# First layer-norm tiles on two engines, and a new token order, in a fused S4 and feed-forward kernel

## The chip, the cores and the metric

The kernel runs on one core of a Trainium2 chip. The metric is device microseconds from launch to end, the median of several executions; lower is better. A profiled execution gives the trace that the views below are read from. Engines are named as in the profile: PE is TensorE (matmul), PEld its weight loads, DVE is VectorE, ACT is ScalarE, POOL is GpSimd, SP is SyncE, which here only issues DMAs. Every engine runs its own instructions in program order and waits in place for what the next one needs.

## The reference

A block of 2048 tokens of width 512 is normalised. One branch is a state-space convolution (S4) along the tokens, the other a feed-forward network with a hidden width of 1792. The second, through SiLU, gates the first:

```python
xn = _layernorm(x, axis=-1)
s = _A_ref(xn, A_re, A_im, B_re, B_im, C_re, C_im, log_dt, Dskip)   # y = conv(xn, K) + xn * Dskip
g = _silu(_B_ref(xn, w1, b1, w2, b2))                               # gelu(xn w1 + b1) w2 + b2
return x + s * g
...
dt = jnp.exp(log_dt)[:, None]
P = jnp.exp((dt * A)[:, :, None] * l[None, None, :])                # A, B, C complex, 512 x 128
K = jnp.einsum("dn,dnl,dn->dl", Cc, P, dt * Bc).real                # 512 x 2048
```

The convolution goes through a Fourier transform over twice the length.

## The kernel before

**Tiling.** Tokens are taken in tiles of 2 x 128 rows (`ln_load`, `ln_begin`), two tiles to a group of 512 tokens. There are four such groups. The hidden width is 14 blocks of 128, in two halves of 7 (`FA`), so the feed-forward network has 56 steps, one per group and block (`steps`). All matmuls of the network are done in a three-part split: each operand is a rounded high part and a low rest, and high x high, high x low and low x high are added up.

**The layer norm of a group.** VectorE takes mean and variance of each row tile (`ln_stat`, token LS). The inverse square root is worked out by arithmetic on 128x4 numbers (`ln_rsqrt`, line 366; token LR), and VectorE scales each 128x512 row tile (`ln_scale`, line 381; token LC). PE turns it (`ln_turn`, TF), ScalarE rounds the high part `xh` (`ln_high`, TH), and VectorE forms the low part `xl` (`ln_low`, TL). For group 0 all this stands in `prologue`, for the others in the token order.

**The feed-forward steps.** For step j: F.j.0 and F.j.1 are six matmuls each into one of two PSUM buffers named `f1` (`first_half`, lines 287 to 289; step 0 is `first_start`, line 298, and stands in the prologue). G.j is Gelu in place on ScalarE (line 302), H.j the rounding to `hh` on ScalarE (line 307), and R.j the rest `hl` on VectorE (line 313), the last reader of the PSUM buffer. S.j.i, four of them, are three matmuls each into the sums `z` (lines 323 to 325): `hh` x high weight, `hh` x low weight, `hl` x high weight. Weights are loaded by W and WB into a ring of six staging slots; WS.f.0 and WS.f.1 round the high parts on ScalarE, WS.f.2 and WS.f.3 form the low parts on VectorE (line 266), or on GpSimd where a third number 1 is given.

**The S4 kernel's parameters.** Each P.b token takes the next step of the generator `params(b)` for a quarter of the channels. Step 1 (for b = 0 in the prologue) loads six arrays. Step 2 is six products on GpSimd, ending in `wr` and `wi` (lines 519 to 524). Step 3 is two Abs on ScalarE (527, 528). Step 4 is six operations on VectorE (531 to 537). Step 5 is an arc tangent on ScalarE, step 6 ten and more operations on GpSimd, steps 7 to 9 more on VectorE, step 10 a store to memory, from which the tables' loads (KL, `lh`) and then PE's phase products (A, line 617) take them. The time step `dt`, the exponential of a 512-vector, is worked out by `timestep` (lines 491 to 505), 24 small dependent operations on GpSimd. It stands in the prologue, ahead of all P tokens, and `dt` is used from step 7 on.

**The rest.** A, B, C, Z, N, E, Q, U, UD make the convolution kernel, in 32 pieces, beside the feed-forward steps. Behind them come the transforms over four channel quarters (F1, FO, S2, SP, PR, CB, BK, BO, VT, LA), the gate (GM, GA, and for the last quarter SW, SO, LT, GT, AT) and the stores (OS, OT). In `combine`, `gate_add` and `rows_add` a trailing 1 or its absence chooses between VectorE and GpSimd; in `gen_round`, `back_out`, `first_out` and `ln_high` between VectorE and ScalarE.

**What sets the order.** The program is written out under manual scheduling: `prologue()` first, then the 1603 tokens of `ORDER` one after the other. Each engine's queue is the subsequence of the instructions that fall to it. So a token that waits for another engine holds everything behind it on its own engine.

```python
    with tc.manual_schedule():
        prologue()
        for tok in ORDER.split():
            kind, *args = tok.split(".")
            acts[kind](*map(int, args))
```

Of the kernel before, what the change touches and what calls it, by code (L numbers as in the profile page):

```python
# [54 lines left out]
TF.2.1 B.0.1 C.0 S.4.0 WS.6.0 TH.2.1 TF.3.0 WS.6.1 P.0 TL.2.1 WS.6.2 LS.5.0 WS.5.1 S.4.1 P.1 A.1 F.5.0 F.5.1
B.1.1 P.0 S.4.2 TH.3.0.1 TL.3.0 P.1 C.1 TF.3.1 S.3.3 N.0.0 G.5 LD.2 LD.3 P.0 S.4.3 H.5 TH.3.1 LS.4.0 R.5
KL.2.0 LS.5.1 TL.3.1 F.6.0 LS.4.1 KL.0.1 BB F.6.1 F.7.0 WS.6.3 WS.5.3 LR.4 LK.1 KL.1.1 KL.3.0 Z.0 N.0.1
S.5.0 S.5.1 KL.2.1 F.7.1 G.6 A.2 E.0.0 H.6 N.1.0 N.1.1 S.5.2 R.6 F.8.0 WB.8 G.7 LC.4 Z.1 E.0.1 H.7 S.6.0
E.0.2 F.8.1 O.0.0 E.1.0 S.6.1 B.2.1 S.5.3 R.7 G.8 S.6.2 H.8 E.1.1 S.7.0 F.9.0 C.2 LD.4 KL.3.1 Z.2 O.0.1 A.3
R.8 S.6.3 N.2.0 F.9.1 KL.4.0 G.9 O.0.2 S.7.1 E.1.2 H.9 S.8.0 B.3.1 S.8.1 P.1 C.3 LK.0 TF.4.0 N.2.1 O.0.3  # L60
S.7.2 S.8.2 Q.0 R.9 LC.5 TH.4.0 E.2.0 TL.4.0 TF.4.1 E.2.1 S.7.3 E.2.2 TH.4.1 S.8.3 N.3.0 S.9.0 KL.5.0 F.10.0
U.0 P.1 N.3.1 Z.3 S.9.1 LL.6 KL.4.1 A.4 F.10.1 KL.5.1 B.4.1 TL.4.1 G.10 S.9.2 E.3.0 F.11.0 LD.5 F.11.1 P.1
E.3.2 H.10 W.10 G.11 S.9.3 C.4 R.10 A.5 TF.5.0 H.11 S.10.0 E.3.1 TH.5.0 B.5.1 R.11 LS.6.0 S.10.1 C.5 Z.4
N.4.0 OK.0 KL.6.0 N.5.0 KL.7.0 TL.5.0 F.12.0 P.1 F.12.1 S.10.2 G.12 H.12 S.11.0 Z.5 S.11.1 TF.5.1 R.12 N.4.1
Q.1 P.1 S.12.0 P.1 P.1 S.10.3 U.1 KL.6.1 N.5.1 TH.5.1 P.1 F.13.0 E.4.0 LL.7 S.12.1 P.2 TL.5.1 F.13.1 E.5.0
S.11.2 F.14.0 S.11.3 G.13 F.14.1 E.4.2 E.5.1 S.12.2 H.13 R.13 UD.0 P.1 S.12.3 S.13.0 F.15.0 E.4.1 KL.7.1
LS.7.0 A.6 B.6.1 UD.1 F.15.1 E.5.2 G.14 S.13.1 Z.6 LS.7.1 H.14 O.1.0 C.6 G.15 R.14 N.6.0 H.15 LS.6.1 S.13.2
S.13.3 A.7 B.7.1 O.1.1 P.1 O.1.3 F.16.0 F.16.1 KL.8.0 C.7 S.14.0 N.6.1 R.15 P.2 Z.7 O.1.2 S.14.1 S.15.0 LR.6
F.17.0 S.14.2 Q.2 OK.1 F.17.1 E.6.0 G.16 LC.7 H.16 R.16 S.14.3 LC.6 U.2 S.16.0 KL.8.1 S.15.1 N.7.0 E.6.1
# [1097 lines left out]
```

## Time and profile before

| | |
|---|---|
| median of 3 runs | 530.98 us (530.38 to 534.08) |
| profiled execution | 529.94 us |
| its span, first to last instruction | 528.0 us |
| TensorE clock granted, mean | 0.996 |
| VectorE, ScalarE, GpSimd busy | 441.9, 373.2, 242.5 us |

A row of the timeline or of the groups has the start (timeline), the duration in us, the engine, the line of the kernel, the operation, what it writes and reads, sizes, and in brackets how long its engine stood idle before it and what ended that. A row of busy time by stretches has the stretch, its length, then busy time and instruction count of PE, PEld, DVE, ACT and POOL, then the granted clock of TensorE (1.00 is full), the busy share of the DMA engines and GB/s. A row of the waits has the waiting instruction, what it waited for, the total in us, how often, and the longest. A row of the chain of waits has start, duration and what the chain ran through. Instruction ends of pipelined matmuls are modelled, so distances between starts are the better measure for them.

### The profile page before, as it was taken

How to read it: one execution, taken by the hardware profiler on the slowest of the kernel's cores; microseconds unless marked ns; L12 is line 12 of the kernel's file. 1: busy time of each engine (PE TensorE's matmuls, PEld its weight loads, DVE VectorE, ACT ScalarE, POOL GpSimd, SP SyncE). 2: the span in 40 equal slices, each digit the busy share in tenths (PEclk: the TensorE clock that was granted, in tenths of full speed). 3: DMA queues.
4: the chain of work that ended last, by engine and by line, in shares of the span. 5: the costliest groups of instructions: out<-in, count | busy, mean ns of one | idle time of the engine just before them, and what ended most of it. 6: DMA issues, size and time to landing. Idle time of an engine off the chain costs nothing.

```text
span 528.0 us, 16480 instructions
## 1 busy us (share of the span) xinstructions
PE 513.2 (97%) x6931; PEld 417.1 (79%) x6931; DVE 441.9 (84%) x695; ACT 373.2 (71%) x530; POOL 242.5 (46%) x343
## 2 busy tenths in 40 slices
PE   6999999999999999999999999999999999999994
PEld 6786777877777777777777787777888998998972
DVE  5999999999999898999877867988455599788886
ACT  2689888977978898997697898998644543343321
POOL 5637379084531848927345157621303112733250
PEclk9999999999999999999999999999999999999998
DMA  8858823437167182624435155949489457573656
GB/s 224 272 176 276 309 90 135 149 110 269 33 221 253 54 242 72 228 89 127 157 107 196 39 179 117 253 118 115 151 284 187 129 184 122 155 189 88 171 145 165
DMA packets 106345, 86.84 MB, mean 164 GB/s; under 512 B 40974, under 2 KB 84640, under 8 KB 106272
## 3 DMA queue, kind: packets, MB, share of 16 engines
q1 hardware_dynamic: 104736, 84.74, 55.4%
q10 hardware_dynamic: 1472, 1.05, 0.8%
q8 instruction: 54, 0.88, 0.7%
q14 instruction: 19, 0.16, 0.1%
q0 software_dynamic: 64, 0.01, 0.0%
HBM read 52.23 MB, written 33.55 MB: 162 GB/s over the span
## 4 chain that ended last, share of the span: by engine, by line
PE 91%; DVE 3%; DMA 3%; ACT 1%; SPq 1%; issue 0%; ACTq 0%; DVEq 0%
PE s L938 11%; PE z L323 10%; PE f L287 10%; PE z L325 10%; PE z L324 9%; PE f L288 9%; PE f L289 9%; PE s L915 6%; PE kg L678 6%; PE sa L975 6%; PE ph L617 2%; DMA w2s<-in_B_w_dram 2%; PE y L1036 1%; DMA x<-in_A_u_dram 1%; PE xT L403 1%; DMA out_dram<-xb 0%
## 5 line engine op out<-in xcount | busy, mean ns | idle before, releaser
L323 PE MATMUL z<-w2h,hh 128*128 128x512 f32 x224 | 92.0, 411 | 0.0
L287 PE MATMUL f<-xh,w1h 128*128 128x512 f32 x220 | 88.9, 404 | 0.3 <-DVE hl L313 0.2
L325 PE MATMUL z<-w2h,hl 128*128 128x512 f32 x224 | 88.6, 396 | 0.0
L324 PE MATMUL z<-w2l,hh 128*128 128x512 f32 x224 | 88.5, 395 | 0.0
L639 POOL TENSOR_TENSOR mm<-mm,rc 128x32 f32<-128x32 f32 (+4 forms) x125 | 83.2, 666 | 9.8
L289 PE MATMUL f<-xh,w1l 128*128 128x512 f32 x220 | 86.4, 393 | 0.3 <-DVE w1l L266 0.3
L288 PE MATMUL f<-xl,w1h 128*128 128x512 f32 x220 | 86.2, 392 | 0.0
L636 POOL COPY mm<-rc 128x32 f32<-128x32 f32 x25 | 8.8, 352 | 116.6 <-DVE e L666 41.6
L302 ACT ACTIVATE f<-f,b1s 128x512 f32<-128x512 f32 x56 | 37.0, 661 | 23.7 <-PE f L289 19.6
L323 PEld LDWEIGHTS z<-w2h,hh 128*128 128x128 f32 x224 | 42.1, 188 | 12.8 <-issue 3.9
L287 PEld LDWEIGHTS f<-xh,w1h 128*128 128x128 f32 x220 | 41.3, 188 | 13.2 <-issue 2.7
L662 DVE TENSOR_TENSOR e<-mm,ra 128x1024 f32<-128x1024 f32 x32 | 40.3, 1259 | 13.5 <-PE kg L678 9.2
L945 ACT COPY uh<-s 128x512 f32<-128x512 f32 x30 | 17.6, 587 | 46.7 <-PE s L938 39.7
L325 PEld LDWEIGHTS z<-w2h,hl 128*128 128x128 f32 x224 | 42.1, 188 | 10.1
L289 PEld LDWEIGHTS f<-xh,w1l 128*128 128x128 f32 x220 | 41.3, 188 | 10.1 <-DVE w1l L266 1.0
L324 PEld LDWEIGHTS z<-w2l,hh 128*128 128x128 f32 x224 | 42.2, 188 | 8.2
L288 PEld LDWEIGHTS f<-xl,w1h 128*128 128x128 f32 x220 | 41.4, 188 | 8.4
L313 DVE TENSOR_TENSOR hl<-f,hh 128x512 fp32r<-128x512 f32 x56 | 38.3, 683 | 10.6 <-ACT hh L307 10.3
L953 DVE TENSOR_TENSOR t<-s,uh 128x512 f32<-128x512 f32 x56 | 35.9, 680 | 11.7 <-ACT uh L945 11.3
L629 DVE SCALAR_TENSOR_TENSOR ra<-ra,ph 128x1024 f32<-128x1024 f32 x32 | 38.9, 1217 | 6.6 <-ACT ra L623 6.2
L666 DVE TENSOR_TENSOR e<-mm,ra 128x1024 f32<-128x1024 f32 x32 | 40.9, 1282 | 0.0
L647 ACT ACTIVATE ra<-ra 128x1024 f32<-128x1024 f32 x32 | 33.8, 1057 | 5.3 <-DVE ra L629 5.3
(207 smaller groups left out, 1112.9 us busy)
## 6 DMA issues: line engine op xcount, KB each, us to landing
xs<-x SPq DMA_DIRECT2D x8, 512.0 KB
xt_h<-xh SPq DMA_DIRECT2D x4, 1024.0 KB
xt_l<-xl SPq DMA_DIRECT2D x4, 1024.0 KB
za<-zo SPq DMA_DIRECT2D x4, 1024.0 KB
kgd<-ko SPq DMA_DIRECT2D x16, 256.0 KB
xh<-xt_h SPq DMA_DIRECT2D x4, 1024.0 KB
xl<-xt_l SPq DMA_DIRECT2D x4, 1024.0 KB
zi<-za SPq DMA_DIRECT2D x4, 1024.0 KB
```

Of the source, the lines that this page charges most:

```text
L287: PE.matmul(p, wh[:, k, :], xh[:, k, :], start=(k == 0), stop=False)
L288: PE.matmul(p, wh[:, k, :], xl[:, k, :], start=False, stop=False)
L289: PE.matmul(p, wl[:, k, :], xh[:, k, :], start=False, stop=(k == KD - 1))
L313: V.tensor_sub(hl, hf, hh)
L323: PE.matmul(z, hh[:, s], wh, start=(f0 == 0), stop=False)
L324: PE.matmul(z, hh[:, s], wl, start=False, stop=False)
L325: PE.matmul(z, hl[:, s], wh, start=False, stop=(f0 == FA - 1))
L629: V.scalar_tensor_tensor(ra[:, 0], ra[:, 1], MAGIC, p, op0=ALU.subtract, op1=ALU.subtract)
L639: eng.tensor_mul(mv[:, :, 0:3:2, w:2 * w], mv[:, :, 0:3:2, 0:w], rc[:, 2 + 2 * i:4 + 2 * i, :].rearrange("p j c -> p c j").unsqueeze(3).to ...
L662: V.tensor_mul(e1, m1.unsqueeze(1).to_broadcast([P, 2, CH, N1]), ra[:, :, :, :N1])
L666: V.tensor_mul(e2[:, :, :, :H], m2[:, :, :H].unsqueeze(1).to_broadcast([P, 2, CH, H]), ra[:, :, :, dn])
L938: PE.matmul(p[ka * 64:(ka + 1) * 64, r, o, :, jj], mc[h, k, ((0, 2), (1, 0))[c][o], :], xf[b][h, c, :, k, :], start=(c == 0), stop=(c == 1 ...
```

## The change

Four things are done. The memset of `ident` is put ahead of that of `dsk`. For group 0, moments are kept per tile of 256 tokens, and the inverse root of the first tile is worked out on GpSimd by a new function of 12 operations on 128x2, with its two scalings of 128x512 on GpSimd as well. This stands in the prologue ahead of the time-step chain. The root of the second tile, on 128x2, and its two scalings stay on VectorE. And `ORDER` is replaced by another order of the same 1603 tokens, in which about a twentieth have another engine.

The part that falls behind the prologue, up to the second matmul group of step 0, read by engine in the new order: ScalarE WS.1.0, WS.2.0, WS.1.1, WS.2.1, WS.3.0, P.0 (step 3), G.0, H.0; VectorE LS.2.0, LS.3.1, WS.0.3, WS.1.2, LS.3.0, P.0 (step 4), R.0; PE F.1.0, F.1.1, S.0.0, S.0.1, F.2.0, F.2.1. In the old order: ScalarE WS.1.0, P.0 (step 3), G.0, WS.2.0, H.0; VectorE LS.2.0, WS.1.2, P.0 (step 4), R.0; PE F.1.0, F.1.1, F.2.0, S.0.0, S.0.1, F.2.1.

```diff
 ORDER = """
-W.2 P.0 WS.1.0 P.0 LS.2.0 G.0 WS.1.2 WB.2 WS.2.0 LD.0 P.0 H.0 R.0 W.3 F.1.0 LL.4 WS.1.1 WS.2.2 LD.1 F.1.1
-G.1 WS.0.3 WB.3 W.4 F.2.0 S.0.0 LS.3.1 H.1 LL.5 S.0.1 R.1 F.2.1 WS.3.0 WS.3.2 WS.2.1 S.0.2 LS.3.0 WS.1.3
...
-SP.3.6 CB.3.2.0.1 GM.2.0.0 SP.3.7 BK.3.1.1 PR.3.6.0 PR.3.6.1 GM.2.1.0 BO.3.1.0 BO.3.1.1 GM.2.0.1 CB.3.2.1.1
-CH.3.3.0.0.1 GA.2.0.1 PR.3.7.0 BK.3.2.0 CH.3.3.1.0.1 PR.3.7.1 TX.3.1.31 CH.3.3.1.1.1 CH.3.3.0.1 BH.3.3.1.0
-BO.3.2.1.1 BH.3.3.1.1 BO.3.3.0 BO.3.2.0.1 BO.3.3.1.1 SW.2 VT.3.0.0 SW.3 GA.2.1 SO.2.1 VT.3.0.1 OS.2.1
-SO.2.0.1 LA.3.1 SO.3.0 LT.2 GM.3.0.0 OS.2.0 GM.3.0.1 SO.3.1 GM.3.0.2 GM.3.0.3 AT.0.1 LT.3 OT.0 AT.1.1 GT.3
-OT.1 AT.3.1 GT.2 AT.2.1 OT.3 OT.2
+W.2 LS.2.0 WS.1.0 LS.3.1 WS.2.0 WS.1.1 P.0 WB.2 W.3 WS.2.1 WS.3.0 P.0 WS.0.3 WS.1.2 G.0 LS.3.0 D F.1.0 H.0
+F.1.1 P.0 WB.3 R.0 S.0.0 S.0.1 WS.2.2 WS.1.3 G.1 P.0 WS.3.1 W.4 H.1 F.2.0 P.0 F.2.1 S.0.2 LS.2.1 LD.1 LD.0
...
+S2.3.7 CB.3.2.0.1 GM.2.0.1 BK.3.1.1 GM.2.1.1 SP.3.7 GA.2.0 PR.3.6.1 PR.3.6.0 CH.3.3.0.0.1 CB.3.2.1
+CH.3.3.1.0.1 PR.3.7.1 BO.3.1.0.1 BK.3.2.0 PR.3.7.0 CH.3.3.0.1 BO.3.1.1 BH.3.3.1.0 CH.3.3.1.1.1 BO.3.2.1.1
+BH.3.3.1.1 BO.3.3.1.1 BO.3.2.0 TX.3.1.31 BO.3.3.0 VT.3.0.0 SW.2 GA.2.1 VT.3.0.1 SW.3 OS.2.1 LA.3.1 GM.3.0.0
+SO.2.1 GM.3.0.2 SO.2.0 GM.3.0.1 SO.3.1 SO.3.0 OS.2.0 GM.3.0.3 AT.0.1 LT.2 LT.3 GT.2 GT.3 AT.3.1 AT.2.1 AT.1
+OT.0 OT.1 OT.3 OT.2
 """
@@ -227,11 +227,12 @@
     mag = keep.tile([P, 1], F32, name="mag")
     V.memset(mag, MAGIC)
     dsk = keep.tile([P, NB, DB], F32, name="dsk")
-    GP.memset(dsk, 0.0)
     b1s = keep.tile([P, NF], F32, name="b1s")
     fc = keep.tile([P, P], F32, name="fc")
     ident = keep.tile([P, P], F32, name="ident")
-    make_identity(nc, ident)
+    GP.memset(ident, 0.0)
+    GP.memset(dsk, 0.0)
+    make_identity(nc, ident, nomemset=True)
 
     W = {}
 
@@ -363,8 +364,7 @@
         for i in range(2):
             ln_stat(n, i, mv)
 
-    def ln_rsqrt(mv, rs, name):
-        k = TB
+    def ln_rsqrt(mv, rs, name, k=TB):
         va = wka.tile([P, TB], F32, tag="va", name=f"va{name}")[:, :k]
         V.tensor_scalar(va, mv[:, :, 1], eps, -0.5, op0=ALU.add, op1=ALU.mult)
         V.tensor_scalar(rs.bitcast(I32), va.bitcast(I32), -0.5, 519526879.0, op0=ALU.mult, op1=ALU.add)
@@ -378,10 +378,26 @@
         V.scalar_tensor_tensor(t2, t2, 3.375, va, op0=ALU.mult, op1=ALU.mult)
         V.scalar_tensor_tensor(rs, t2, 2.25, rs, op0=ALU.add, op1=ALU.mult)
 
-    def ln_scale(n, mv, rs):
+    def ln_root_first(mv, rs):
+        va, t = (wka.tile([P, 2], F32, tag=m, name=m + "p") for m in ("vap", "t2p"))
+        GP.tensor_scalar(va, mv[:, :, 1], eps, -0.5, op0=ALU.add, op1=ALU.mult)
+        GP.tensor_scalar(rs.bitcast(I32), va.bitcast(I32), -0.5, 519526879.0, op0=ALU.mult, op1=ALU.add)
+        GP.tensor_mul(t, rs, rs)
+        GP.tensor_mul(t, t, va)
+        u = wka.tile([P, 2], F32, tag="t3p", name="t3p")
+        GP.tensor_scalar(u, t, 5.0 / 3.0, 1.0, op0=ALU.add, op1=ALU.mult)
+        GP.tensor_mul(u, u, t)
+        GP.tensor_scalar(u, u, 1.25, 1.0, op0=ALU.add, op1=ALU.mult)
+        GP.tensor_mul(rs, u, rs)
+        GP.tensor_mul(t, rs, rs)
+        GP.tensor_mul(t, t, va)
+        GP.tensor_scalar(t, t, 3.375, 2.25, op0=ALU.mult, op1=ALU.add)
+        GP.tensor_mul(rs, t, rs)
+
+    def ln_scale(n, mv, rs, eng=None):
         x = ln[n]
         for i in range(2):
-            V.tensor_scalar(x[:, i, :], x[:, i, :], mv[:, i, 0:1], rs[:, i:i + 1],
+            (eng or V).tensor_scalar(x[:, i, :], x[:, i, :], mv[:, i, 0:1], rs[:, i:i + 1],
                             op0=ALU.subtract, op1=ALU.mult)
 
     def ln_store(n):
@@ -709,6 +725,16 @@
         warm(7)
         next(step)
         warm(14)
+        halves = [(wka.tile([P, 2, 2], F32, tag=f"mvp{n}", name=f"mvp{n}"),
+                   wka.tile([P, 2], F32, tag=f"rsp{n}", name=f"rsp{n}")) for n in range(2)]
+        for n in range(2):
+            ln_stats(n, halves[n][0])
+        ln_root_first(*halves[0])
+        split(0, 0)
+        split(0, 1)
+        ln_rsqrt(*halves[1], "0", 2)
+        ln_scale(0, *halves[0], GP)
+        ln_scale(1, *halves[1])
         for _ in step:
             pass
         stage_first(1)
@@ -717,14 +743,6 @@
         for n in range(2, 4):
             ln_load(n)
         SY.dma_start(cbs, cb)
-        mv, rs = pair(0)
-        ln_stats(0, mv[:, 0:2, :])
-        ln_stats(1, mv[:, 2:4, :])
-        split(0, 0)
-        split(0, 1)
-        ln_root(0)
-        for n in range(2):
-            ln_scale(n, *moments(n))
         for q, tag in enumerate(("ph", "z", "z", "z")):
             ln_turn(q // 2, q % 2, tag)
             ln_high(q // 2, q % 2)
```

More of the change, by code (lines that the diff above doesn't have):

```diff
@@ L55 @@
[L55 to L69, printed above, removed]
@@ new lines @@
+BK.1.2.0 CB.1.3.0 OS.0.0 S2.2.0 BO.1.2.0.1 S2.2.1 TG.1.0 GA.0.1.1 SP.2.0 BO.1.2.1.1 CB.1.3.1.1 F1.3.0.0.1
+FO.3.0.0.0 F1.3.0.1.0 SP.2.1 SK.3 FO.3.0.0.1.1 FO.3.0.1.0.1 F1.3.0.2.1 FO.3.0.1.1 TG.1.1.18 BK.1.3.0
+FO.3.0.2.0 PR.2.1.0 FO.3.0.2.1.1 F1.3.0.3.1 PR.2.0.0 PR.2.0.1 PR.2.1.1 S2.2.2 BO.1.3.1.1 FO.3.0.3.1.1
+BO.1.3.0 VT.1.0.0 CB.2.0.0 TX.1.0.17 FO.3.0.3.0 S2.2.3 SP.2.2 PR.2.2.1 VT.1.1.0 SP.2.3 PR.2.3.0 OS.0.1
+CB.2.0.1.1 F1.3.1.0.0 FO.3.1.0.0 FO.3.1.0.1 PR.2.2.0 BK.2.0.1 F1.3.1.1.0 VT.1.0.1 VT.1.1.1 BO.2.0.0
```

176 lines of the change are left out of this document (93 added, 83 removed).

## The prediction

> **What bounds the kernel now.** I read the page first, then busy time by stretches of the span, then what PE waited for, then the chain of waits in the first 30 us, then the timeline.
>
> ```profile
> PE 513.2 (97%) x6931; PEld 417.1 (79%) x6931; DVE 441.9 (84%) x695; ACT 373.2 (71%) x530; POOL 242.5 (46%) x343
> ```
>
> ```profile
> 17.00:36.00 19.00, 18.51 (x81) 14.27 (x80) 18.17 (x47) 13.45 (x22) 8.21 (x15) 1.00 0.72 229
> 36.00:50.00 14.00, 13.41 (x65) 9.73 (x63) 13.48 (x26) 13.30 (x28) 11.34 (x19) 1.00 0.72 226
> 50.00:375.00 325.00, 324.91 (x3319) 252.55 (x3319) 287.57 (x419) 281.37 (x347) 167.59 (x238) 1.00 0.50 152
> 375.00:514.00 139.00, 137.60 (x3304) 125.43 (x3304) 102.47 (x161) 56.91 (x120) 43.77 (x36) 1.00 0.65 170
> 514.00:528.00 14.00, 6.05 (x95) 3.28 (x92) 9.26 (x15) 2.38 (x4) 1.34 (x1) 0.85 0.71 169
> ```
>
> ```profile
> PE ph L617 <- DMA lh<-pcd: 0.6, 1, 0.6
> ...
> PE f L287 <- DVE hl L313: 0.2, 1, 0.2
> ```
>
> PE is the bound. Outside the first 17 us and the last 14 it idles 0.49, 0.59, 0.09 and 1.40 us in the four middle stretches, 2.57 us together. From 50 to 375 us there is nothing left to win, and a microsecond that PE loses before 50 us comes out at the end, unless those gaps or the tail give it back. So the first thing to ask of the change is when PE gets its early work. The chain of waits at the start (start, duration, what) answers it:
>
> ```profile
> 12.34 4.61 DMA w2s<-in_B_w_dram
> 16.97 0.74 DVE w1l L266
> 17.76 0.28 DVE pr_ci L531
> ...
> 19.94 0.69 DVE hl L313
> 20.68 0.50 PE f L287
> ```
>
> PE's third block of the first product (token F.2.0, line 287, at 20.68) needs the PSUM buffer that block 0 frees when VectorE has formed `hl` (R.0, line 313, ended 20.62). Directly ahead of R.0 on VectorE stand the six operations of parameter step P.0 number 4 (lines 531 to 537), and they need ScalarE's two Abs (number 3), which need GpSimd's `wr` and `wi` (number 2). The list of PE's waits shows the join: 0.2 us on `hl`. So GpSimd's queue at the start is on the path of PE, although GpSimd is only 46% busy.
>
> ```profile
> 6.80 0.18 DVE L360 BATCH_NORM_AGGREGATE mv<-bst 128x2 f32<-128x6 f32 x1
> ...
> 7.00 0.25 POOL L491 TENSOR_SCALAR sm_x<-sm_x 128x4 f32<-128x4 f32 x1 [3.97 <-ACT b1s L488]
> ...
> 10.52 0.20 POOL L500 TENSOR_TENSOR sm_e<-sm_e,sm_r 128x4 f32<-128x4 f32 x1
> ...
> 14.03 0.46 POOL L519 TENSOR_TENSOR pr_wr<-pr_cr,pr_br 128x128 f32<-128x128 f32 x1
> ...
> 16.15 0.68 DVE L359 BATCH_NORM_STATS2 bst<-x 128x6 f32<-128x512 f32 x1
> ...
> 16.82 0.47 POOL L524 TENSOR_TENSOR pr_wi<-pr_wi,pr_m 128x128 f32<-128x128 f32 x1
> ...
> 17.33 0.31 ACT L528 ACTIVATE pr_cr<-pr_wi 128x128 f32<-128x128 f32 x1 [0.66 <-POOL pr_wi L524]
> ...
> 17.54 0.64 ACT L302 ACTIVATE f<-f,b1s 128x512 f32<-128x512 f32 x1
> ...
> 18.74 0.58 ACT L307 CAST hh<-f 128x512 fp32r<-128x512 f32 x1
> ```
>
> GpSimd works without a pause from 7.00 (first operation of the time-step chain) to 17.29 (`wi`): chain 7.03 us, then six products of 3.26 us. ScalarE's second Abs starts 0.04 us behind it.
>
> **The change, part by part.**
>
> *Root on GpSimd.* Added ahead of the time-step chain: 12 operations on 128x2. They can begin when the second tile row's moments are there, 6.98 (row at 6.80), which is when the chain began before; GpSimd's idle time ahead of 7.00 can't be used. Price: the first 12 small operations of the chain took 10.52 - 7.00 = 3.52 us, with the same VectorE work beside them. So the root ends near 10.5.
>
> *Two scalings of 128x512 on GpSimd.* The trace has no such operation. Rows that bound it:
>
> ```profile
> 9.09 0.19 POOL L498 TENSOR_SCALAR sm_e<-sm_r 128x4 f32<-128x4 f32 x1
> ...
> 11.11 0.49 POOL L500 TENSOR_TENSOR sm_e<-sm_e,sm_r 128x4 f32<-128x4 f32 x1
> ...
> 13.05 0.20 POOL L500 TENSOR_TENSOR sm_e<-sm_e,sm_r 128x4 f32<-128x4 f32 x1
> ...
> 23.19 0.30 POOL L549 TENSOR_SCALAR pr_h<-pr_h 128x128 f32<-128x128 f32 x1
> ...
> 34.40 1.31 POOL L266 TENSOR_TENSOR w2l<-w2s,w2h 128x512 fp32r<-128x512 f32 x1 [6.71 <-ACT w2h L264]
> ```
>
> ```profile
> 11.01 1.92 DVE L384 TENSOR_SCALAR x<-x,mv,rs 128x512 f32<-128x512 f32 x4
> ```
>
> A TENSOR_SCALAR took 0.19 us at 4 elements and 0.30 at 128, so 0.9 ns per element and 0.63 us at 512: the low end. The high end is the two-input operation of the same size, 1.31 us. I take the slope, since the operation has one tensor input, but the rows also show GpSimd slowed while VectorE scales (11.01 to 12.93): the operations from 11.11 to 13.05 are four at L500 and L501 that took 1.94 us where four at 0.29 would take 1.17, a factor of 1.65. The second scaling meets VectorE's scaling of tile 1 (11.0 to 12.0): 0.63 x 1.65 = 1.04. Together 1.7 us, bounds 1.3 and 2.6. [...] The trace shows slowing by two thirds, not a stop.
>
> *The memsets.* `ident` is cleared ahead of `dsk`, so the warm-up matmuls may begin a little earlier. They end ahead of the transposes, which wait for the statistics and the scalings: nothing.
>
> *What that does to the first tiles.* Row 0 is scaled near 11.15 instead of 11.55, row 1 near 12.2 instead of 12.0, rows 2 and 3 near 11.5 and 12.0 on VectorE instead of 12.5 and 12.9. VectorE keeps a root of its own with the same count of operations. The first product therefore starts within 0.3 us of before. I cost this at nothing: PE waits for `hl` later in any case; with that cover gone it would be worth at most 0.4 us either way.
>
> *What is queued behind on GpSimd.* The chain (7.03) and the products (3.26) are unchanged and follow in order: 3.52 + 1.7 = 5.2 us later. `wi` is ready at 17.29 + 5.2 = 22.5 and the second Abs ends at 22.85.
>
> *What is queued behind the Abs.* In the new order ScalarE has five weight casts, then the Abs pair, and only then Gelu (G.0) and the cast `hh` (H.0) of block 0. VectorE has LS.2.0, LS.3.1, WS.0.3, WS.1.2, LS.3.0, then P.0 number 4, then R.0. VectorE's own queue would be through near 20.2: 16.15 where the last `xl` ended, three statistics of 0.82 (16.15 to 16.97 before), two subtractions of 0.79 (16.97 to 17.76). So GpSimd binds: number 4 from 22.95, and R.0, which ended at 20.62, ends at 25.8. `hh`, ended at 19.32, is there near 24.0 (Gelu 0.64 and cast 0.58 behind the Abs).
>
> *What PE has in the meantime.* F.0 and F.1, no more: F.2 needs the buffer that R.0 frees. The new order sends S.0.0 and S.0.1 ahead of F.2, but each block's third matmul needs `hl`.
>
> ```profile
> 17.00 0.40 PE L287 MATMUL f<-xh,w1h 128*128 128x512 f32 x1
> 17.23 0.40 PE L288 MATMUL f<-xl,w1h 128*128 128x512 f32 x1
> 17.90 0.50 PE L289 MATMUL f<-xh,w1l 128*128 128x512 f32 x1 [0.27 <-DVE w1l L266]
> ```
> ```profile
> 20.68 0.50 PE L287 MATMUL f<-xh,w1h 128*128 128x512 f32 x1 [0.22 <-DVE hl L313]
> ...
> 25.10 0.39 PE L323 MATMUL z<-w2h,hh 128*128 128x512 f32 x1
> ```
>
> Before, the 18 matmuls of F.2 and S.0.0, S.0.1 ran from 20.68 to 25.10. After, two of them can go at 24.0 and 16 wait for `hl` at 25.8: at 0.23 us each (17.00 to 17.23 before, at lines 287 and 288) they end at 29.5. PE is 4.4 us late. That is the main term: bounds 3.9 (scalings at 0.63) and 5.3 (at 1.31).
>
> *The parameter chain behind it.* Numbers 6 to 10 follow number 4, so the table phase A.0 moves by about the same 4.5 us; its place in PE's order is the same, and it waited 0.6 us for `lh` already. I add 0.3, between -0.6 and +1.0. SP's queue takes the skip loads and the stores LD.0, LD.1 in another order. W.3, which the fifth cast ahead of the Abs needs, can go when VectorE's `w1l` of block 0 frees its slot, near 15; with the 4.61 us to landing of the load at 12.34 it is there near 20, while the Abs waits for GpSimd until 22.5: nothing, and up to 1 us if GpSimd were that quick.
>
> *Middle.* The same 1603 tokens in another order, with the engine changed on about a twentieth. PE's work is the same; PE has no gap that could close beyond 1.4 us, and new gaps can open. I take 0, bounds -1.4 and +1.5.
>
> *Tail.*
>
> ```profile
> 509.61 1.23 DVE L1047 TENSOR_TENSOR xb<-gb,xb 128x1024 f32<-128x1024 f32 x1
> ...
> 512.80 2.54 POOL L1047 TENSOR_TENSOR xb<-gb,xb 128x1024 f32<-128x1024 f32 x1
> ...
> 520.39 1.29 DVE L1090 TENSOR_TENSOR last<-last 128x512 f32<-128x512 f32 x2
> ...
> 523.64 0.69 DVE L1090 TENSOR_TENSOR last<-last 128x512 f32<-128x512 f32 x1
> ```
>
> VectorE ends the kernel. One add of 128x512 (AT.1, half of the row at 520.39, 0.65 us) moves to GpSimd, beside the last two multiplications, which takes it off VectorE's chain. The add GA.2.0 of 1.23 us goes to GpSimd as well (2.5 us there by the row at 512.80), ahead of the halves of the last combine: it can hold them by up to 1.3 us. I take -0.6, bounds -1.2 and +1.3.
>
> **Sum.** The profiled execution took 529.94 us (span 528.0 and 1.94 around it): 529.94 + 4.4 + 0.3 + 0 - 0.6 = 534.0. The median of the runs shown, 530.98, stands 1.04 above that execution, so on the median's footing the forecast is 535.1 us, 4.1 us or 0.8% slower. About 1% (5.3 us, 536.3) is what a measurement can tell from no change.
>
> **The rivals.**
>
> *PE's clock falls during the new wait.* PE would idle from about 21.9 (F.1, whose third matmul waits for `w1l` near 19.4, has ten left) to 24.0, 2.1 us, and again 1.3 us before `hl`. The end of the trace shows what idling does to the granted clock (seventh figure, behind POOL):
>
> ```profile
> 520.00:521.00 1.00, 0.96 (x6) 0.08 (x2) 0.97 (x4) 0.00 (x0) 0.00 (x0) 1.00 0.89 248
> ...
> 523.00:524.00 1.00, 0.00 (x0) 0.00 (x0) 0.96 (x3) 0.00 (x0) 0.00 (x0) 0.87 0.93 223
> 524.00:525.00 1.00, 0.00 (x0) 0.00 (x0) 0.34 (x1) 0.00 (x0) 0.00 (x0) 0.50 0.95 244
> ```
>
> The last matmul ended at 520.96; a mean of 0.87 in the slice from 523 to 524 puts the fall to 0.50 at 523.74, 2.8 us later. The wait of 2.1 us falls short by 0.7; from a GpSimd 0.7 us slower on, it decides. If the clock takes as long to come back as to fall (an estimate), 2.8 us at half speed cost 1.4 us, and together with the 0.7 the time is 535.1 + 2.1 = 537.2, slower by more than 1%. [...]
>
> *VectorE's queue, not GpSimd, sets R.0.* This is the case that ends not slower. It needs GpSimd's addition to be under 2.5 us. R.0 would end at 20.2 + 2.18 + 0.68 = 23.05, PE 1.6 us late, less 0.6 at the tail: 530.98 + 1.0 = 532.0, and 530.6 if the middle's gaps close too. Against it stand the 12 dependent operations, which alone take 3.5 us by the row at 10.52.
>
> *A new gap in the transform half.* A combine or a copy moved to the slower engine holds PE's next matmuls: +1.3 in the tail by the row at 512.80 instead of -0.6, so 535.1 + 1.9 = 537.0. For it: GpSimd's add now stands ahead of the last combine. Against it: VectorE is relieved by 1.23 us just there.
>
> **How the numbers follow.** Forecast (start 3.9 to 5.3 late, the rest -1.2 to +0.8) 0.65, own range 533.5 to 536.8; clock falls 0.12; VectorE's queue sets it 0.11; a new gap 0.12. Slower by over 1% are the second and most of the fourth and a tenth of the forecast: 0.29. Faster by over 1% would need the start's loss gone and 5 us won where PE idles 2.6: 0.02. The rest, 0.69, is within 1%. The range leaves out the lower half of the VectorE case and the upper ends of the two slow ones: 531.8 to 538.0, forecast 535.1.
>
> **What would show it.** In the changed profile: the first TENSOR_SCALAR of the time-step chain near 12.2 instead of 7.00; `wi` near 22.5; ScalarE's second Abs waiting for POOL, and Gelu behind it near 22.8; R.0 ending near 25.8; PE idle about 4 us more between 17 and 26, put down to `hh` and `hl`; the stretch from 50 to 375 as full as before; the last add on VectorE one place shorter. I am wrong if the scalings on GpSimd are far from 0.6 to 1.1 us, if Gelu runs before 20 us, or if PE is on its second product by 22 us.

## The result, and the profile after

| | before, measured beside it | changed |
|---|---|---|
| median of 4 runs | 531.33 us (530.38 to 534.08) | 538.74 us (537.24 to 540.00) |
| profiled execution, span | 529.94, 528.0 us | 538.31, 536.5 us |
| TensorE clock, mean | 0.996 | 0.989 |

The ratio on record is 1.0105, 95% interval 1.0075 to 1.0136; the two medians of four stand further apart, by 7.4 us or 1.4%. The changed kernel is slower by 1 to 1.4%. Against the median the forecast of 535.1 us was 3.6 us too low, and the median lies 0.7 us above the top of its range; by the ratio, 1.0105 x 530.98 = 536.6 us, it was 1.5 us too low and inside the range. The sign was right; the size was too small.

Busy time on the page of the changed kernel:

```profile
PE 516.5 (96%) x6931; PEld 418.1 (78%) x6931; DVE 456.6 (85%) x720; ACT 368.5 (69%) x522; POOL 241.4 (45%) x340
```

And by stretches of its span, columns as in the prediction:

```profile
17.00:36.00 19.00, 15.89 (x72) 12.66 (x71) 14.45 (x31) 12.81 (x23) 13.19 (x36) 0.92 0.56 184
36.00:50.00 14.00, 13.53 (x63) 10.39 (x62) 12.69 (x39) 10.40 (x23) 4.29 (x9) 1.00 0.37 106
50.00:375.00 325.00, 324.81 (x3203) 250.95 (x3201) 297.06 (x438) 280.51 (x350) 163.58 (x231) 1.00 0.51 158
375.00:514.00 139.00, 138.14 (x3254) 123.78 (x3256) 110.23 (x166) 55.47 (x111) 41.64 (x31) 1.00 0.63 163
```

From 50 us on PE is as full as before, so the loss is to be sought ahead of it. Between 17 and 36 us PE is busy for 15.89 us instead of 18.51. Rows picked from the timeline of the first 50 us say on what it waits:

```profile
7.61 0.26 POOL L383 TENSOR_SCALAR vapp<-mvp,eps 128x2 f32<-128x2 f32 x1 [4.58 <-DVE mvp L361]
11.06 4.18 POOL L400 TENSOR_SCALAR x<-x,mvp,rsp 128x512 f32<-128x512 f32 x2
11.24 1.34 DVE L400 TENSOR_SCALAR x<-x,mvp,rsp 128x512 f32<-128x512 f32 x2
13.23 1.12 PE L419 MATMUL xT<-ident,x 128*128 128x128 f32 x4 [3.31 <-POOL x L400]
15.33 0.25 POOL L507 TENSOR_SCALAR sm_x<-sm_x 128x4 f32<-128x4 f32 x1
24.99 0.45 POOL L540 TENSOR_TENSOR pr_wi<-pr_wi,pr_m 128x128 f32<-128x128 f32 x1
25.48 0.31 ACT L544 ACTIVATE pr_cr<-pr_wi 128x128 f32<-128x128 f32 x1 [0.64 <-POOL pr_wi L540]
25.70 0.64 ACT L303 ACTIVATE f<-f,b1s 128x512 f32<-128x512 f32 x1
27.01 0.50 PE L324 MATMUL z<-w2h,hh 128*128 128x512 f32 x1 [2.03 <-ACT hh L308]
28.01 0.68 DVE L314 TENSOR_TENSOR hl<-f,hh 128x512 fp32r<-128x512 f32 x1
28.75 0.50 PE L326 MATMUL z<-w2h,hl 128*128 128x512 f32 x1 [1.01 <-DVE hl L314]
48.08 0.39 PE L633 MATMUL ph<-cbs,lh 48*128 48x512 bf16 x1 [0.15 <-DMA lh<-pcd]
```

The chain is the one that was forecast: GpSimd's root (7.61 to 11.06), its two scalings, the time-step chain from 15.33, `wi` at 25.44, Abs, Gelu at 25.70, R.0 ending at 28.69 instead of 20.62, and PE waiting 2.03 us for `hh` and 1.01 for `hl`. One row is off: the two scalings took 4.18 us, where 1.7 was in the sum. A.0's second matmul, at 40.70 before, stands at 48.08: 7.38 us of the loss are there.

A wait of 3.31 us ahead of the first transposes is new. What it did to PE's clock (seventh figure, behind POOL) is in the stretches around it:

```profile
9.92:13.00 3.08, 0.00 (x1) 0.00 (x0) 2.42 (x9) 0.41 (x1) 2.72 (x5) 1.00 0.86 214
13.00:20.00 7.00, 5.82 (x26) 5.30 (x27) 3.62 (x6) 3.60 (x7) 5.72 (x17) 0.51 0.59 209
20.00:25.00 5.00, 4.90 (x25) 3.55 (x23) 3.09 (x8) 1.75 (x4) 4.27 (x14) 1.00 0.55 144
25.00:27.00 2.00, 0.00 (x0) 0.00 (x0) 1.11 (x5) 1.49 (x4) 0.45 (x1) 1.00 1.04 397
```

PE did the transposes and most of step 0's first product at a granted clock of 0.51 on average (13.00 to 20.00), and still had to wait 2.03 us for `hh` behind them.

The end of the changed kernel:

```profile
523.62 1.94 PE L1081 MATMUL w<-ident,Z 128*128 128x128 f32 x16 [0.91 <-DVE Z L1002]
528.81 1.77 POOL L1108 TENSOR_TENSOR last<-last 128x512 f32<-128x512 f32 x1 [4.90 <-DVE last L1061]
529.48 4.18 SPq L1112 DMA_DIRECT2D out_dram<-last  x8
529.49 4.38 ACTq L1112 DMA_DIRECT2D out_dram<-last  x8
530.69 1.29 DVE L1108 TENSOR_TENSOR last<-last 128x512 f32<-128x512 f32 x2
```

and the same places before:

```profile
515.25 1.94 PE L1063 MATMUL w<-ident,Z 128*128 128x128 f32 x16 [0.91 <-DVE Z L984]
521.11 4.12 SPq L1094 DMA_DIRECT2D out_dram<-last  x8
521.11 4.31 ACTq L1094 DMA_DIRECT2D out_dram<-last  x8
```

From the first of these matmuls to the first store it is 5.86 us in both, and from there to the end 6.89 us before, 7.02 after. VectorE's last add now ends 2.50 us behind the first store issue (531.98) instead of 3.22 (524.33). That gained nothing: on each of two queues eight stores are issued in a row, about 0.5 us apart, and these rows end 1.1 us behind the last add before (521.11 + 4.31 = 525.42) and 1.9 us behind it after (533.87).

### The profile page after: what moved, and what is told of

It reads as the page before. It is cut to its first block, busy times and chain, and to the rows that moved or that the text cites. A ratio compares the mean times of both kernels' runs of the same rounds, so it can differ in the third digit from the quotient of the medians.

```text
span 536.5 us, 16520 instructions
## 1 busy us (share of the span) xinstructions
PE 516.5 (96%) x6931; PEld 418.1 (78%) x6931; DVE 456.6 (85%) x720; ACT 368.5 (69%) x522; POOL 241.4 (45%) x340
## 3 DMA queue, kind: packets, MB, share of 16 engines
q10 hardware_dynamic: 1472, 1.05, 0.8%
## 4 chain that ended last, share of the span: by engine, by line
PE 83%; DVE 4%; DMA 4%; POOL 3%; SPq 2%; issue 1%; ACT 1%; DVEq 0%; ACTq 0%; POOLq 0%
PE s L956 10%; PE z L324 10%; PE f L288 9%; PE z L326 9%; PE z L325 9%; PE f L290 8%; PE f L289 8%; PE s L933 6%; PE kg L694 5%; PE sa L993 5%; PE ph L633 2%; PE y L1054 1%; DMA x<-in_A_u_dram 1%; PE xT L419 1%; DMA w2s<-in_B_w_dram 1%
## 5 line engine op out<-in xcount | busy, mean ns | idle before, releaser
L324 PE MATMUL z<-w2h,hh 128*128 128x512 f32 x224 | 93.4, 417 | 2.0 <-ACT hh L308 2.0
L288 PE MATMUL f<-xh,w1h 128*128 128x512 f32 x220 | 87.8, 399 | 0.0
L655 POOL TENSOR_TENSOR mm<-mm,rc 128x32 f32<-128x32 f32 (+4 forms) x115 | 77.5, 674 | 9.0
L652 POOL COPY mm<-rc 128x32 f32<-128x32 f32 x23 | 12.0, 524 | 119.6 <-DVE e L685 53.1
```

Source lines behind the costliest of these rows:

```text
L288: PE.matmul(p, wh[:, k, :], xh[:, k, :], start=(k == 0), stop=False)
L324: PE.matmul(z, hh[:, s], wh, start=(f0 == 0), stop=False)
L655: eng.tensor_mul(mv[:, :, 0:3:2, w:2 * w], mv[:, :, 0:3:2, 0:w], rc[:, 2 + 2 * i:4 + 2 * i, :].rearrange("p j c -> p c j").unsqueeze(3).to ...
```

## The experiments

The theory (G): GpSimd's queue delays `wi`; Abs, step 4 and R.0 follow it, and PE follows R.0. Rivals: the order of tokens is the loss (O); the clock that falls at the first transposes is the loss (C); the transposes' own wait is the loss (T). Stamps are from the profiled executions, ratios from the timed runs.

| kernel | `wi` ends | R.0 ends | first matmul of A.0 | span | ratio to before (95%) |
|---|---|---|---|---|---|
| before | 17.29 | 20.62 | 39.73 | 528.0 | |
| changed | 25.44 | 28.69 | 47.54 | 536.5 | 1.0105 (1.0075 to 1.0136) |
| order only | 17.06 | 22.75 | 41.26 | 530.8 | 0.9980 (0.9957 to 1.0003) |
| prologue only | 24.71 | 27.95 | 48.95 | 540.9 | 1.0153 (1.0088 to 1.0217) |
| scalings on VectorE | 21.10 | 24.35 | 44.41 | 533.0 | 1.0014 (0.9988 to 1.0040) |
| spare scalings | 25.13 | 28.37 | 48.28 | 537.4 | 1.0154 (1.0106 to 1.0201) |
| steps 3, 4 behind R.0 | 25.55 | 23.55 | 47.83 | 535.9 | 1.0096 (1.0071 to 1.0120) |
| 12 fillers more | 24.52 | 27.77 | 49.05 | 539.2 | 1.0144 (1.0094 to 1.0193) |
| 26 fillers more | 24.73 | 27.97 | 46.44 | 544.2 | 1.0302 (1.0260 to 1.0344) |
| scaling by constants | 24.80 | 28.04 | 49.06 | 537.3 | 1.0124 (1.0089 to 1.0160) |
| last add on VectorE | 25.12 | 28.37 | 49.23 | 537.7 | 1.0140 (1.0094 to 1.0186) |
| `wi` inside the chain | 15.20 | 20.23 | 39.41 | 530.2 | 0.9998 (0.9974 to 1.0021) |
| order, and `wi` inside | 14.83 | 22.96 | 41.47 | 530.9 | 0.9981 (0.9959 to 1.0004) |

The profiled execution of before was one of its shorter ones: 529.94, while its medians beside the experiments were 532.01 to 532.36. So spans are compared among the experiments, and ratios with before. The changed kernel's ratio comes from its own four runs; by medians (538.74 and 539.20 us) it and the kernel with the last add on VectorE are alike, although the ratios read 1.0105 and 1.0140.

The table ties A.0 to R.0. From the end of R.0 to A.0 it is 18.5 to 19.2 us in the six kernels whose clock was full from R.0 to A.0 (before, changed, order only, 26 fillers, and the two with `wi` inside), and 19.9 to 21.3 us in the six whose clock was at half for a while behind it. Only the kernel with steps 3 and 4 behind R.0 is outside both.

**The order alone, and the prologue alone.** The diff of the changed kernel, taken in halves: for the first the old prologue with the new `ORDER`, for the second the reverse.

> The old prologue (root and all scalings of group 0 on VectorE) with the new token order. Theory G (GpSimd's queue holds the parameter step ahead of R.0, and behind it the phase product A.0): GpSimd is as early as before, wi near 17.3; VectorE's longer queue sets R.0, ending near 23.0; the second matmul of A.0 near 43.1 to 43.7 (40.7 before); the whole 2 to 3 us slower than before. Rival O (the new order loses the time by itself, in the middle or at the end): 7 us or more slower, with A.0 near 41.

> The new prologue (root and scalings of the first tile on GpSimd) with the old token order. Theory G: wi near 25.4, R.0 ending near 28.5, F.2.0 behind it near 28.5 instead of 20.7; the whole 7.5 to 9.5 us slower than before. Rival O: within 2 us of before.

The order alone costs nothing that can be measured (531.36 us), though R.0 ends 2.1 us later. Theory G had forecast 2 to 3 us here, and A.0's second matmul at 43.1 or later; it came at 41.83. PE's waits of the kernel with the order alone (waiting instruction, what it waited for, total, times, longest):

```profile
PE f L289 <- DVE w1l L266: 1.7, 2, 1.4
PE z L325 <- DVE hl L313: 0.9, 1, 0.9
```

The prologue alone costs 1.5%, in an interval that overlaps that of the whole change. Rival O falls. Between the order alone and the whole change only the prologue differs: `wi` is 8.4 us later, R.0 5.9, A.0 6.3, and the median 7.4 us longer.

**The scalings back on VectorE, the root left on GpSimd.**

```diff
-        ln_scale(0, *halves[0], GP)
+        ln_scale(0, *halves[0])
```

> The changed kernel with the two scalings of the first tile on VectorE, its root still on GpSimd. Theory G: GpSimd's queue is 4.2 us shorter, wi near 21.2, R.0 near 24.5, A.0 near 43.9 to 44.5, the whole about 4 us faster than the changed kernel and 3.5 to 4.5 slower than before. Rival C (the slow scalings hold PE's first transposes, the clock falls, and that is the loss): no idle of 3 us and no half clock ahead of the first product, and then the whole within 1 us of before. Rival O: 7 us slower than before still.

534.38 us, 4.4 less than the changed kernel. Against before it is 0.7 us longer by the ratio, which the interval doesn't tell from none, and 2.0 us by the medians; G had forecast 3.5 to 4.5, rival C under 1, so this kernel by itself doesn't decide between them. The rows of this kernel's timeline that answer to 15.33 and 48.08 above:

```profile
10.44 0.28 POOL L507 TENSOR_SCALAR sm_x<-sm_x 128x4 f32<-128x4 f32 x1
44.41 0.57 PE L633 MATMUL ph<-cbs,lh 48*128 48x512 bf16 x2
```

By medians, the root's 12 operations cost 3.0 us against the order alone (531.36), and the two scalings 4.4 us against this kernel. But the edit takes away three things at once: the delay of the queue, the transposes' wait and the clock's fall at them. The next one parts these.

**Two spare scalings.** The kernel just told of, with two more scalings on GpSimd at the place where the change has them, into a buffer that is loaded at 49 us and not read by anything else earlier. It is cleared first, ahead of the root, at 2.96 for 0.54 us, when GpSimd had nothing to do. GpSimd's queue is delayed; the transposes wait for nothing.

```diff
+        GP.memset(b2b, 0.0)
...
         ln_scale(0, *halves[0])
+        for i in range(2):
+            GP.tensor_scalar(b2b, b2b, halves[0][0][:, i, 0:1], halves[0][1][:, i:i + 1],
+                             op0=ALU.subtract, op1=ALU.mult)
```

> The kernel whose four first scalings are all on VectorE (534.4 us, root on GpSimd), with two further scalings of 128x512 on GpSimd at the place where the change has them, into a buffer that is not read until it is loaded much later. GpSimd's queue is then that of the changed kernel, but the transposes do not wait for it. Theory G (what counts is the delay of the queue behind the scalings): wi ends 4.2 us later than 21.1, R.0 near 28.5, time 538 to 539, as the changed kernel. Rival T (what counts is that the first transposes wait for GpSimd and the clock falls there): 534 to 535, as without the two.

539.62 us, as slow as the changed kernel, and R.0 at 28.37. Rival T falls: with transposes as early as before, and the clock full until 24.75, the loss is all there. PE's longest wait is now the one for `hh`:

```profile
PE z L324 <- ACT hh L308: 5.3, 1, 5.3
```

and with that the clock falls there, by stretches, so that a part of this kernel's loss is the clock's, but behind the wait and not at the transposes:

```profile
21.00:24.00 3.00, 0.35 (x2) 0.00 (x0) 0.00 (x0) 0.00 (x0) 2.52 (x10) 1.00 1.02 386
24.00:25.00 1.00, 0.00 (x0) 0.00 (x0) 0.00 (x0) 0.31 (x1) 0.92 (x3) 0.88 0.18 74
25.00:31.00 6.00, 3.79 (x8) 2.59 (x9) 5.36 (x13) 5.76 (x9) 2.79 (x7) 0.50 0.03 9
```

**Fillers ahead of the transposes.** These kernels keep PE busy while it waits for the first scaled row.

```diff
-        warm(14)
+        warm(40)
```

> The changed kernel with 26 more filler matmuls on PE ahead of its first transposes, so that PE does not stand idle for the 3.31 us before 13.23. Theory G (GpSimd's queue sets R.0): the granted clock stays near 1.00 from 13 to 20 and F.1 ends about 2 us earlier than its 25.0, but R.0 still ends at 28.5 to 28.9, PE's waits for hh and hl grow by what the products gain, and the time is within 1 us of the changed kernel's 538.7. Rival C (the fallen clock is the loss): the time falls by 1.5 to 2.5 us. If the fillers run into the transposes, xT starts later than 13.23 and both lose by that.

The 26 fillers ran until 16.2, past the first scaled row. The clock stayed at 1.00 from there beyond A.0, and R.0 (27.97) and A.0 (46.44) were earlier than in the changed kernel, by 0.7 and 1.1 us. So with no fall of the clock at all up to that point A.0 still came 6.7 us later than before (39.73):

```profile
30.00:46.00 16.00, 16.00 (x74) 13.05 (x73) 13.72 (x42) 11.54 (x25) 5.49 (x12) 1.00 0.55 170
```

Yet the kernel took 547.97 us: PE stopped three times far behind, at 171, 300 and 336 us, for 1.2, 1.7 and 3.6 us. The timeline has no releaser for these:

```profile
333.98 1.99 PE L694 MATMUL kg<-e,e 128*32 128x64 f32 x127
339.58 0.32 PE L694 MATMUL kg<-e,e 128*32 128x64 f32 x1 [3.61 <-issue]
```

The stop lies between the 127th and the 128th of a run of like matmuls. In all three stops the DMA engines were busy throughout (shares of 1.08, 1.05 and 1.00); that is a coincidence in time, and the cause is open. The clock fell behind the longest one, at 338.55. So the whole time says nothing on C, and the fill was made again with 12, `warm(26)`.

> The changed kernel with 12 more filler matmuls (0.25 us each, as the 26 of the longer fill took 6.4 us) ahead of PE's first transposes, so that they end near 12.9, where the first scaled row is ready. Theory G (GpSimd's queue sets R.0): granted clock 1.00 from 13 to 20, the first product ends about 2 us earlier, R.0 where GpSimd lets it (27.9 to 28.7), time within 1 us of the changed kernel's 538.7, unless PE stops in its stream again as it did in the longer fill. Rival C (the fallen clock is the loss): 1.5 to 2.5 us faster than the changed kernel.

The clock was full throughout the first product, which was done 1.2 us earlier than in the changed kernel. The time was 540.43 us, none the better. The stretches show why:

```profile
22.00:24.00 2.00, 1.83 (x8) 1.15 (x7) 0.03 (x1) 0.31 (x1) 1.91 (x5) 1.00 0.95 273
24.00:26.00 2.00, 0.00 (x0) 0.00 (x0) 1.03 (x5) 1.41 (x4) 0.45 (x1) 1.00 1.05 421
26.00:27.00 1.00, 0.74 (x2) 0.30 (x2) 0.97 (x2) 0.98 (x3) 0.00 (x0) 1.00 0.46 184
28.00:34.00 6.00, 6.00 (x15) 4.64 (x16) 4.00 (x7) 2.50 (x4) 5.18 (x11) 0.50 0.66 223
```

PE got earlier to the wait for `hh` (2.25 us), and the clock fell to 0.50 behind that wait, where PE has all its work before it. Rival C falls as the cause, by A.0 in the kernel with 26 fillers and by the spare scalings; this time alone would not show it, since the clock fell later instead. In the changed kernel the fall at the transposes lay under the wait for R.0 and was covered. With 12 fillers the fall behind that wait was not: A.0 came 1.5 us later than in the changed kernel with R.0 0.9 us earlier.

**Steps 3 and 4 behind R.0.** The parameter steps are taken out of the way of the Gelu and of R.0 in the changed kernel's order.

```diff
-... WS.3.0 P.0 WS.0.3 WS.1.2 G.0 LS.3.0 D F.1.0 H.0
-F.1.1 P.0 WB.3 R.0 S.0.0 S.0.1 WS.2.2 WS.1.3 G.1 P.0 WS.3.1 W.4 H.1 F.2.0 P.0 ... G.2 R.1
+... WS.3.0 WS.0.3 WS.1.2 G.0 LS.3.0 D F.1.0 H.0
+F.1.1 WB.3 R.0 S.0.0 S.0.1 WS.2.2 WS.1.3 G.1 H.1 R.1 P.0 P.0 P.0 WS.3.1 W.4 F.2.0 P.0 ... G.2
```

> The changed kernel with parameter steps 3 and 4 (two Abs, six VectorE operations) moved behind Gelu, hh and hl of blocks 0 and 1. Theory G has two halves. If the wait at R.0 alone costs the time: R.0 ends near 24, F.2.0 starts near 26 instead of 29.8, the whole 3.4 us faster than the changed kernel. If the parameter chain behind it stands in series: R.0 is as early, but PE waits 4 to 5 us for lh at A.0, which stays at 48 or comes up to 1.2 us later, and the whole is the changed kernel's time or up to 1.2 us more. Rival C: no gain, and no wait at A.0 beyond 1 us.

R.0 ended at 23.55 and PE waited neither for `hh` nor for `hl`; the kernel took 537.77 us, 1 us less than the changed one. What was won came back further on:

```profile
34.95 0.35 DVE L570 SCALAR_TENSOR_TENSOR pr_ci<-pr_ci,sm_dt,pr_br 128x128 f32<-128x128 f32 x1 [0.90 <-POOL pr_br L567]
40.02 0.68 DVE L267 TENSOR_TENSOR w1l<-w1s,w1h 128x512 fp32r<-128x512 f32 x1
40.76 0.80 PE L290 MATMUL f<-xh,w1l 128*128 128x512 f32 x1 [2.67 <-DVE w1l L267]
```

VectorE's parameter steps 7 to 9 wait for GpSimd's step 6 and begin at 34.95, no earlier than in the changed kernel (35.28). Behind them in VectorE's queue is the low half of a weight that PE needs. GpSimd's delay reaches PE in two places, one behind the other; to clear the first of them was worth 1 us by the medians. A.0 stayed at 47.83, as the second half of G had it, but not by the wait that G named: PE waited 2.67 us for this weight, none for `lh`, and the clock was at half from 40.27 for 3.4 us.

**Scaling by constants.** GpSimd's two scalings subtract 0 and multiply by 1; the first 256 tokens are left without their normalisation.

```diff
+            m, r = (0.0, 1.0) if eng else (mv[:, i, 0:1], rs[:, i:i + 1])
+            (eng or V).tensor_scalar(x[:, i, :], x[:, i, :], m, r, op0=ALU.subtract, op1=ALU.mult)
```

> The changed kernel with GpSimd's two scalings of the first token tile taking the constants 0 and 1 in place of the mean and root columns, so the first 256 tokens are not normalised. Theory (the two operands that differ from partition to partition make the 2.09 us of one): 0.5 to 1.0 us each, the time-step chain starts 2.2 to 3.2 us earlier than 15.33, R.0 ends 2 to 3 us earlier than 28.69, and the time is 2 to 3 us under the changed kernel's. Rival (the size makes it, or f32 through GpSimd at 128x512 as such): 2.0 to 2.1 us each and no change in the time.

By the view of that line (count, then shortest, median and longest in ns) one still takes 2.03 us:

```profile
L401 POOL TENSOR_SCALAR x<-x x2: 1921/2031/2141, 10.3 to 12.4; 128x512 f32<-128x512 f32 x2
```

My theory of the two column operands falls; the kernel took 538.91 us. What is left is the size, or f32 of that size on GpSimd as such; no run parts these.

**The last add back on VectorE.** In the changed kernel's order `AT.1` becomes `AT.1.1`, behind `AT.0.1`.

> The changed kernel with one token changed at the end: the last block's add AT.1 on VectorE behind that of block 0, as before the change, in place of GpSimd. Theory (the stores' issues in a row set the end): from the first swing matmul to the end 12.9 us as before, the time within 0.3 us of the changed kernel's. Rival, my tail term (VectorE's last adds set the end): 0.65 us longer behind the first swing matmul.

The timeline of the end has the matmul and VectorE's last adds at

```profile
524.66 1.94 PE L1081 MATMUL w<-ident,Z 128*128 128x128 f32 x16 [0.91 <-DVE Z L1002]
532.32 1.29 DVE L1108 TENSOR_TENSOR last<-last 128x512 f32<-128x512 f32 x2
```

VectorE's adds end 8.95 us behind that matmul, in the changed kernel 8.36; to the end of the kernel it is 13.0 and 12.9 us. So the place of that add sets 0.2 us at most; the time of 539.20 us is 0.5 above the changed kernel's, where 0.3 was allowed. This kernel starts as the changed one does, instruction for instruction, so it is a second profile of the same start. Its root began 0.6 us earlier, and the clock went another way:

```profile
13.00:20.00 7.00, 5.69 (x28) 5.23 (x26) 4.14 (x8) 4.16 (x8) 5.55 (x18) 0.51 0.60 205
26.70:33.60 6.90, 6.35 (x14) 4.61 (x15) 5.87 (x10) 4.37 (x6) 4.94 (x10) 0.51 0.47 156
```

Here the clock falls a second time, at the wait for `hh` (2.29 us), and A.0 comes 1.7 us later than in the changed kernel's own profile, with R.0 0.3 us earlier. So the second fall costs 2.0 us at A.0. The changed kernel's timed executions fit that: they took 537.24, 538.31, 539.18 and 540.00 us at mean clocks of 0.992, 0.989, 0.990 and 0.985, where 6.8 us at half are worth 6.8 x 0.5 / 536.5 = 0.006.

**Candidates for a faster kernel.** Nothing of parameter step 2 needs the time step, so its six products can stand in the middle of the time-step chain:

```diff
+            if c == 1.0 / 6:
+                yield
...
-        for _ in step:
-            pass
+        next(step)
...
+        next(pgen[0])
+        for _ in step:
+            pass
```

> The kernel before with only its parameter step 2 moved: the six products that end in wr and wi stand in the middle of GpSimd's time-step chain in place of behind it. Nothing of step 2 uses the time step. Theory (R.0 follows GpSimd's queue through wi): wi ends 3 to 4 us earlier than 17.29, R.0 about as much earlier up to what its Gelu allows (19.5 to 20.3 in place of 20.62), PE's wait ahead of F.2.0 goes; the parameters themselves come no earlier, since step 7 needs the time step: 0 to 1 us faster than before (ratio 0.998 to 1.000). Rival: what is won at R.0 comes back in front of A.0, ratio 1.000.

> The prologue of before, with parameter step 2 in the middle of the time-step chain, in the new order: a candidate for the fastest. Theory: in the new order alone R.0 ended at 22.75 and PE waited for w1l and hl; with wi 3 us earlier the Abs pair does not hold ScalarE's Gelu, R.0 ends 1 to 2 us earlier and A.0 comes 0 to 1 us earlier than 41.8: ratio to before 0.995 to 0.999. Rival: what is won comes back ahead of A.0, ratio 0.998 to 1.000.

In the old order `wi` came 2.1 us earlier instead of 3 to 4, and R.0 only 0.4: VectorE now waited for ScalarE's `hh`. PE's wait ahead of F.2.0 didn't go; it was 0.73 us instead of 0.22. In the new order R.0 did not move at all (22.96 against 22.75 with the order alone), since ScalarE reached the Abs late by its own queue. Neither is faster than before by more than the measurement: no version here beats the kernel before.

## Why the prediction was right in its mechanism and too small in its size

*Root on GpSimd: right.* 3.45 us against 3.52. It began 0.6 us later than taken, because `x` landed later in this execution (the statistics of its second row began at 6.60 instead of 6.07); in the other profiles of the same prologue GpSimd's scalings began between 10.13 and 10.51 instead of 11.06.

*Two scalings on GpSimd: the step that failed.* In the sum 1.7 us, bounds 1.3 and 2.6; measured 4.18. The prediction had named scalings far from 0.6 to 1.1 us as a sign that it is wrong; they took 2.09 each. Of the 2.9 us by which `wi` was later than forecast (25.44 against 22.5), 2.5 are this term; the start adds 0.6, the chain 0.3 (7.33 for 7.03), and the products took 0.5 less. The mistake was in the reading: the 0.30 us at 128 elements was a single row, and the shortest of its kind. The view of the two lines in the kernel before (shortest, median, longest) would have shown it:

```profile
L549 POOL TENSOR_SCALAR pr_h<-pr_h x8: 300/459/1152, 23.2 to 241.4; 128x128 f32<-128x128 f32 x8
L545 POOL TENSOR_SCALAR pr_br<-pr_m x4: 376/879/1159, 21.5 to 236.8; 128x128 f32<-128x128 f32 x4
```

From 0.19 us at 4 elements a line through the first median gives 0.19 + 508 x (0.459 - 0.19) / 124 = 1.3 us at 512 elements, through the second 3.0. The measured 2.09 lies between these, and both ends are above the 0.63 that I took. The factor of 1.65 for VectorE's work beside it was not the cause either: the second scaling ran mostly while VectorE stood idle, and the two took 2.11 and 2.07 us.

*What VectorE's scalings do to it.* The prediction read from the trace of before that GpSimd is slowed by two thirds (a factor of 1.65) beside them, and not stopped. The view of the two spare scalings (shortest, median, longest in ns) tells how much:

```profile
L739 POOL TENSOR_SCALAR b2b<-b2b,mvp,rsp x2: 2072/2397/2722, 10.6 to 13.4; 128x512 f32<-128x512 f32 x2
```

The first ran beside all four of VectorE's (2.20 us from 10.67 on) and took 2.72 us, the second, begun at 13.4, 2.07. So the first took 0.65 us longer; a stop for the whole 2.20 us would have made it 4.27. In the changed kernel the one beside VectorE's two scalings (1.34 us from 11.24 on) took 2.11, the other 2.07. VectorE's own two beside GpSimd's took 0.98 us each with 12 fillers and 0.54 with the prologue alone; what makes that difference no run shows.

*What is queued behind: right.* Chain, products, Abs, Gelu, step 4 and R.0 followed in the order forecast. R.0 with `wi` at 25.44 would be due 3.3 us later, as forecast (22.5 to 25.8), that is at 28.7; it ended at 28.69.

*What PE loses: the formula was right.* Sixteen matmuls at 0.23 us behind R.0 end at 28.69 + 3.7 = 32.4, 7.3 us behind the 25.10 of before. The next matmul, that of S.0.2, did start at 32.51, and the second of A.0 was 7.38 late. With the measured price of the scalings in the sum the forecast would have been 535.1 + 2.5 = 537.6.

*First tiles, costed at nothing.* The first row was scaled at 13.15 instead of 11.15, PE waited 3.31 us, and the clock fell to half at 13.08. The named cover, PE's later wait for `hl`, held all the same: with the two spare scalings the transposes were early and the time as bad.

*The clock, a rival at 0.12.* It was priced at 2.1 us, from a wait at `hh` 0.7 us longer than forecast. Its condition was wrong: it took 2.8 us of idling in a row for what makes the clock fall, but with 12 fillers it fell behind a wait of 2.25 us. That the clock is back after another 2.8 us was my estimate; ahead of A.0 the runs show it at half for 3.42 or 6.83 us. In the profiled execution the clock did not fall there, though the wait was 2.03 us and followed by another of 1.01. In the second profile of the same start it did, behind 2.29 us, at a cost of 2.0 us. So this rival joined the main case in some executions instead of standing against it.

*Parameter chain, +0.3: nearly right.* A.0 is 7.38 us late where R.0 explains 7.3, and PE waited for `lh` for 0.5 us (two waits) instead of 0.6.

*Middle, 0.* From A.0 to the first matmul of the end the profiled loss grows from 7.4 to 8.4 us. It is no more than the spread between executions. From the first matmul of A.0 to the end it is, by the table, 488.3 us before and 489.0 changed, 488.1 to 490.2 in the other kernels of the new order (the one with 26 fillers apart), and 490.8 and 491.9 in the other two of the old order.

*Tail, -0.6: wrong.* Measured +0.1 or less. VectorE's last add was taken for the end of the kernel, but the stores' issues, eight on each queue in a row from the first finished piece on, end behind it. The profile of before had both rows.

## What to carry to other kernels

Before work is moved to an idle engine, read what stands behind it in that engine's queue, and follow it to the bound engine: GpSimd was 46% busy and yet on PE's path. Price an operation by the shortest, median and longest of the nearest groups, not by one row; where the nearest size is a quarter of the wanted one, take the whole spread into the range. A delay of a queue that reaches the bound engine in several places in a row isn't cured at the first of them (steps 3 and 4 behind R.0 won 1 us), and a clock kept up ahead of a wait can fall behind it (with 12 fillers 1.00 up to the wait of 2.25 us, 0.50 behind it).
